# Top-k attention with a squared-ReLU feed-forward: the last batch by quarters, last rows two batches at a time, and attention ahead of older feed-forward work

## The chip, the cores and the metric

The kernel runs on one core of a Trainium2 chip. The metric is the time of one execution in device microseconds (us). A profile of one execution gives the span from the first to the last instruction, which is some microseconds shorter.

## The reference

There are 8 batches, 8 heads, 576 rows and a head width of 64. Each row of attention keeps its 32 largest scores; the result, with the heads side by side, goes through a feed-forward block of 512, 2048 and 512 columns.

```python
def _attn_ref(q, k, v):                       # (8, 8, 576, 64) each
    scores = np.matmul(q, k.transpose(0, 1, 3, 2)) / np.sqrt(64)
    kth = np.partition(scores, -32, axis=-1)[..., -32:-31]
    scores = np.where(scores >= kth, scores, -1000000000.0)
    attn = np.exp(scores - np.max(scores, axis=-1, keepdims=True))
    attn = attn / (np.sum(attn, axis=-1, keepdims=True) + 1e-09)
    return np.matmul(attn, v)

def reference(q, k, v, moe_w_in, moe_w_out):
    x = _attn_ref(q, k, v).transpose(0, 2, 1, 3).reshape(4608, 512)
    r = np.maximum(x @ moe_w_in, 0.0)         # w_in: 512 x 2048
    return (r * r) @ moe_w_out                # w_out: 2048 x 512
```

## The kernel before

**Groups.** Attention is done in 144 groups. A group is 128 query rows of two heads of one batch (a head pair, hp), or, for the rows 512 to 575 (called Z), 64 rows of four heads. A batch has 4 pairs with the row blocks 0 to 3, and two Z groups. For each group:

- TensorE makes the scores s in fp32 (two heads beside each other, 128 x 1152) and ScalarE copies them to SBUF (L541).
- VectorE and GpSimd find the 32nd largest score of each row. VectorE folds each row into the maximum of pairs, m (L597), and of fours, f (first quarter, L607); GpSimd makes the values that were left out by integer addition and subtraction of the bit patterns (L592): a small half of 144 columns (t2, then `mid`) and a large half of 288 columns (t1, then `low`). VectorE takes eight maxima and replaces them, three times over a growing part of f (L624, L628; the replacements need `mid`), and then eight of all of it (kth, L631, which needs `low`). kth is exact unless a check at the very end finds that a row did not fit; then everything is done again in a plainer way, which does not happen with these inputs.
- ScalarE makes a mask w from s and kth (L639), one instruction for each head. TensorE transposes s and adds the mask, scaled to a very large negative number, in PSUM; I call these 18 matmuls the flip. They are L433, tile `ident,s`, and L430, tile `steep_bf,w`. ScalarE takes the exponential (p, L673).
- `collect`, for one or two groups of a pair at once: TensorE multiplies p with v (av, with the sum of each row in a column of its own), ScalarE copies av (L700), VectorE takes the reciprocal of the sum (L702), GpSimd normalizes (x, L704), TensorE transposes x, and ScalarE copies it into its place in xt (L728).

**Chunks.** When all heads of a chunk of rows are in xt, `feed` does the feed-forward block for these rows: 64 first-layer matmuls (tile `xt,win` or `xz,win`), whose outputs fill PSUM banks of 512 columns each, Relu on ScalarE (g, L754), the square on GpSimd (L768) or ScalarE (L771), on VectorE for the last chunk (L765); then for each 128 rows 16 second-layer matmuls of 512 columns (tile `wo,g`), a copy (L788) and a store. Chunks are the rows 0 to 255 and 256 to 511 of a batch, and the last 64 rows of four batches together. The last batch begins with its Z groups, goes on with the row blocks 2 and 3 of all pairs as one chunk, and ends with block 0 and block 1 as chunks of 128 rows.

**The order of the work.** No engine's order is written out by hand. Each operation is handed to a planner with an assumed duration and a priority, a time at which it would be wanted (smaller is sooner). The planner plays the program through with these durations: on each engine, whenever it is free, it takes the ready operation with the smallest priority for which buffers are free. The order that results is fixed in the program; on the chip each engine goes through its own list, and waits on semaphores for what an instruction needs. Priorities are spaced by PER for each group (`tg = T0 + PER * n`). Scores are wanted LEAD before tg, the pair and four maxima ME and MQ before it, the small half MP before it, the flip and what follows at tt. Feed-forward work is wanted from the end of the chunk's attention plus NBO, spaced by STEP, and later by LAG (LAGL in the last batch).

Buffers that matter here: all short-lived PSUM tiles (av, transposes, both feed-forward layers) share two banks, named psum. Scores have three banks, the flip two and a part of a third, and that third bank is shared with a scratch tile of the maxima (sq). In SBUF there are 6 buffers of s, and 4 each of f, w and p.

The lines that set the row order, the chunks and the flip's priority:

```python
seq = [(0, Z), (2, Z)] + [(hp, g) for hp in range(NHP) for g in (2, 3)]   # last batch
return seq + [(hp, g) for g in (0, 1) for hp in range(NHP)], [[0], [1], [2, 3]]
...
if b % 4 == 3:
    CHUNKS.append([(b - 3 + i, 512, 64) for i in range(4)])
CHUNKS += [[(NB - 1, 256, 256)], [(NB - 1, 0, 128)], [(NB - 1, 128, 128)]]
...
tt = tg + PER + 2
```

Of the kernel before, what the change touches and what calls it, by code (L numbers as in the profile page):

```python
# [8 lines left out]
FP32 = mybir.dt.float32  # L9
BF16 = mybir.dt.bfloat16  # L10
I32 = mybir.dt.int32

P = 128
# [278 lines left out]
def bass_top_k_attn__then__act_relu_squared_kernel(  # L292
# [8 lines left out]
    NB, H, S, D = q.shape  # L301
# [4 lines left out]
    NHP = 4  # L306
    NPAIR = NB * NHP
    NBLK = 9
    DM = H * D
    DFF = moe_w_in.shape[1]  # L310
    NFB = DFF // P
    NCT = DM // P
    NALL = NPAIR * NBLK

    def sb(name, shape, dt=FP32, n=None):
# [1 line left out]
            return nc.alloc_sbuf_tensor(name, shape, dt)  # L317
        return [nc.alloc_sbuf_tensor(f"{name}{i}", shape, dt) for i in range(n)]

    PER = 5.52  # L320
    T0 = 12.0
    LEAD = 36.03
    ME = 17.74
    MQ = 18.56
    MP = 5.21
    MA = 21.03
    SQ = 4.72
    WD = 4
    WC = 0
    WA = 2.47  # L330
    WN = 6
    NBO = 8.74
    LAG = 12.01
    STEP = 2.91
    LATE = 1.54
    LAGL = 20

    ident32 = sb("ident32", [P, P])
    ident_bf = sb("ident_bf", [P, P], BF16)
# [3 lines left out]
    NGRP = NALL // 2  # L343
# [17 lines left out]
        "t2": ([P, 2, QUART], FP32, 2), "f": ([P, 2, S], FP32, 4), "a": ([P, 2, 8], FP32, 2),  # L361
        "sh": ([P, 2], FP32, 2), "w": ([P, 2, S], BF16, 4), "p": ([P, 9, 128], BF16, 4),
        "av": ([P, 4, D + 1], FP32, 3), "x": ([P, 4, D], BF16, 2), "xt": ([P, NCT, 256], BF16, 4),
        "xz": ([P, NCT, 256], BF16, 2), "o": ([P, DM], FP32, 2),
    }
    mem = {nm: sb(nm, *spec) for nm, spec in sizes.items()}
    pools = {nm: Pool(nm, spec[2]) for nm, spec in sizes.items()}
# [34 lines left out]

    Z = 4

    def batch_order(b):
        if b < NB - 1:
            seq = [(hp, g) for hp in range(NHP) for g in (0, 1)]
            for hp in range(NHP):
                seq += [(hp, 2), (hp, 3)] + ([(hp - 1, Z)] if hp % 2 else [])
            return seq, [[0, 1], [2, 3]]  # L410
        seq = [(0, Z), (2, Z)] + [(hp, g) for hp in range(NHP) for g in (2, 3)]
        return seq + [(hp, g) for g in (0, 1) for hp in range(NHP)], [[0], [1], [2, 3]]


    CHUNKS = []
    for b in range(NB):
        if b < NB - 1:
            CHUNKS += [[(b, 0, 256)], [(b, 256, 256)]]
        if b % 4 == 3:
            CHUNKS.append([(b - 3 + i, 512, 64) for i in range(4)])  # L420
    CHUNKS += [[(NB - 1, 256, 256)], [(NB - 1, 0, 128)], [(NB - 1, 128, 128)]]

    def two(ap, step, n_):

# [12 lines left out]
    def build(full, weights, pl):  # L437
        state = {"n": 0, "u": 0, "pairs": 0, "last": {}}
# [66 lines left out]
        def top_k(gi, qks, tg):  # L505

            n = state["n"]
# [54 lines left out]
            if full:  # L562
                a, sh = tile("a"), tile("sh")
                for rnd in range(4):
                    src = st if rnd == 0 else f
                    for i in range(2):
                        get = dict(r=[st]) if rnd == 0 else dict(hold=[f])
                        if rnd == 3:
# [4 lines left out]
                                       after=prev[i], take=[a] if rnd == 0 and i == 0 else [],  # L573
# [57 lines left out]
                    ks.append(chain(kth, i, prev[i] + [low], .665, lambda i=i: vec.max(  # L631
                        eighth(kth, i), at(f)[:, i, :]), hold=[f]))
            kths.extend(ks)
            tw = tg + PER
            wt = tile("w")
            if not full:

# [6 lines left out]
            for i in range(2):  # L644
                o = pl.op("gp", .75, tw + 1.3 * i, lambda i=i: gp.tensor_scalar(
                    at(f)[:, i, :], at(st)[:, i, :], kth[:, i, n:n + 1], STEEP, ALU.subtract, ALU.mult),
                    r=[st], hold=[f], after=[ks[i]])
# [86 lines left out]
        def feed(chunk, xt, tm, step):  # L734

            nt = sum(n_ for _, _, n_ in chunk)
            b = chunk[-1][0]
            last, end = b == NB - 1, chunk is CHUNKS[-1]
            kf = max(1, 512 // nt)
            lag = 0 if end else LAGL if last else LAG  # L740
            gs = [tile("g") for _ in range(NFB // kf)]
            for i, g in enumerate(gs):
                hh = Tile(psum)

                def fh(hh=hh, i=i):
                    for f in range(kf):
                        fb = kf * i + f
                        for ct in range(NCT):
                            ins = mm(bank(hh)[:, nt * f:nt * f + nt], win[:, ct, 128 * fb:128 * fb + 128],
                                     at(xt)[:, ct, 0:nt], ct == 0 and f == 0)  # L750
                    return ins

                def fr(hh=hh, g=g):
                    return act.activation(at(g)[:, 0:kf * nt], bank(hh)[:, 0:kf * nt], ACTF.Relu)  # L754

                tf = tm + step * i
                w_ = kf * nt
                ho = pl.op("pe", .03 + kf * 4 * (nt / 2340 + .002), tf + lag, fh, r=[xt], w=[hh], take=[hh, g],
                           after=weights if chunk is not CHUNKS[0] else weights and weights[NCT * (kf * i // 8):][:NCT],
                           nbf=tf if not last else 0)  # L760
                if chunk is CHUNKS[0] and weights:
                    first_h.append(ho)
                pl.op("act", .19 + w_ / 1200, tf + lag + .5, fr, r=[hh], w=[g])
                if end:
                    pl.op("dve", .1 + w_ / 1900, tf + lag + .8, lambda g=g: vec.tensor_tensor(  # L765
                        at(g)[:, 0:w_], at(g)[:, 0:w_], at(g)[:, 0:w_], ALU.mult), u=[g])
                elif last or i * SQ % 8 < SQ:
                    pl.op("gp", .15 + w_ / 480, tf + lag + 1, lambda g=g: gp.tensor_tensor(  # L768
                        at(g)[:, 0:w_], at(g)[:, 0:w_], at(g)[:, 0:w_], ALU.mult), u=[g])
                else:  # L770
                    pl.op("act", .19 + w_ / 1200, tf + lag + 1, lambda g=g: act.activation(  # L771
                        at(g)[:, 0:w_], at(g)[:, 0:w_], ACTF.Square), u=[g])
            for tb in range((nt + 127) // 128):
                n_ = min(128, nt - 128 * tb)
                op_, ob = Tile(psum), tile("o")
                to = tm + step * (len(gs) + 1 + 4 * tb)
                for sub in range(4):
                    def fo(sub=sub, op_=op_, tb=tb, n_=n_):
                        for fb in range(4 * sub, 4 * sub + 4):
                            c = nt * (fb % kf) + 128 * tb  # L780
                            ins = mm(bank(op_)[0:n_, :], at(gs[fb // kf])[:, c:c + n_], wo[:, fb, :], fb == 0)
                        return ins

                    pl.op("pe", .9, to + lag + step * sub, fo,
                          r=sorted({gs[fb // kf] for fb in range(4 * sub, 4 * sub + 4)}, key=lambda t: t.num),
                          w=[op_], take=[op_, ob] if sub == 0 else [], after=weights[8 + 2 * sub:10 + 2 * sub], order=[ho],
                          nbf=to + step * sub if not last else 0)
                pl.op("act", .6, to + lag + 4 * step, lambda op_=op_, ob=ob, n_=n_: act.copy(  # L788
                    at(ob)[0:n_, :], bank(op_)[0:n_, :]), r=[op_], w=[ob])
                rows, at_ = [], 0  # L790
                for b_, r0, m_ in chunk:
                    lo_, hi_ = max(at_, 128 * tb), min(at_ + m_, 128 * tb + n_)
                    if lo_ < hi_:
                        rows.append((lo_ - 128 * tb, hi_ - lo_, S * b_ + r0 + lo_ - at_))
                    at_ += m_
                pl.op("sp", 2.3, to + lag + 4 * step + 1, lambda ob=ob, rows=rows: [nc.sync.dma_start(
                    out[row:row + m_, :], at(ob)[p0:p0 + m_, :]) for p0, m_, row in rows],
                    r=[ob], ndma=len(rows), sem=lambda o: f"o{o.tiles[0].slot}")
# [13 lines left out]
        for b in range(NB):  # L812
            seq, stages = batch_order(b)
            pairs, held = {}, {}
            last = b == NB - 1
            for hp, gi in seq:
                tg = T0 + PER * state["n"]
                hps = (hp, hp if gi != Z else hp + 1)
                for x in hps:
                    if x not in pairs:  # L820
                        pairs[x] = load_pair(b, x, tg)
                st, wt = top_k(gi, [pairs[x][0] for x in hps], tg)
                tt = tg + PER + 2
                pt = attend(gi, st, wt, tt)
                js = [gi] if gi == Z else [g for g in stages if gi in g][0]
                held.setdefault((hp, js[0]), []).append((pt, [pairs[x][1] for x in hps]))
                if gi != js[-1]:
                    continue
                r0, n_ = 128 * js[0], 128 * len(js) if gi != Z else 64
                i, col = place(b, r0, n_)  # L830
                first = xts[i] is None
                if first:
                    xts[i] = tile("xz" if len(CHUNKS[i]) > 1 else "xt")
                collect(gi, held[hp, js[0]], (xts[i], col, first), hp, tt)
                left[i] -= n_ * (2 if gi == Z else 1)
                if left[i] == 0:
                    tm = T0 + PER * state["n"] + (NBO if not last else 8)
                    c = CHUNKS[i]
                    feed(c, xts[i], tm, (STEP if b < NB - 2 else 1.9) if not last else (1.5 if c is not CHUNKS[-1] else .5))
# [63 lines left out]
    early, pre, zeros, weights = setup(main)  # L903
# [3 lines left out]
    n = 0  # L907
# [79 lines left out]
```

## Time and profile before

| | before |
|---|---|
| time, median of 3 runs | 878.67 us (878.38 to 881.07) |
| span of the profile | 875.4 us |
| mean granted TensorE clock | 0.987 |
| busy: TensorE, VectorE, ScalarE, GpSimd | 809.3, 824.4, 765.1, 787.2 us |
| TensorE, second layer (`wo,g`, 128x512) | 379 ns mean of one |
| VectorE, kth (L631, 128x576) | 747 ns mean, 288 times |
| GpSimd, large half (L592, 128x576) | 1412 ns mean, 144 times |
| ScalarE, exponential (L673, 128x1152) | 1134 ns mean, 144 times |

In the profile PE is TensorE's matmuls and PEld its weight loads, DVE is VectorE, ACT is ScalarE, POOL is GpSimd, SPq is the queue that issues the transfers. The mean of one instruction is its whole duration: instructions overlap on their engine, so that a row of them takes less than their number times the mean. In a timeline a line holds several instructions of one kind that follow each other (x4); the number behind the start is the time from the start of the first to the end of the last. What stands in square brackets is idle time of the engine before the line, and what ended it. The change moves every line number after it by 14; the text names operations by their tiles.

### The profile page before, as it was taken

To read this page: it belongs to the slowest core of one execution; us is meant where nothing else is said; L and a number is where in the kernel's file an instruction comes from. 1 tells how busy PE (TensorE), PEld (TensorE's weight loads), DVE (VectorE), ACT (ScalarE), POOL (GpSimd) and SP (SyncE) were. 2 spreads that over 40 slices of the span, in tenths; PEclk is the share of its full clock that TensorE was granted. 3 is DMA by queue.
4 is the path that set the end of the run, shared out by engine and by line. 5 is a ranking of instruction groups with operands and counts; after the bars stand their busy time and mean duration, and the time that the engine had idled before them with its cause. 6 is when DMAs were issued, how large, how long until landed. Compare 5 with 4: busy or idle time off the path is not lost.

```text
span 875.4 us, 22041 instructions
## 1 busy us (share of the span) xinstructions
PE 809.3 (92%) x7726; PEld 608.3 (69%) x7778; DVE 824.4 (94%) x3409; ACT 765.1 (87%) x1254; POOL 787.2 (90%) x821
## 2 busy tenths in 40 slices
PE   4777999999999999998999999999999999999996
PEld 3556767667776777766677677776777676777674
DVE  2899999999999999999999999999999999999951
ACT  4798988899998998889989889898999899898873
POOL 6888999999999889998999969999999989999962
PEclk9699999999999999999999999999999999999999
DMA  8982112031210213011320032101321030000101
GB/s 182 214 217 76 42 28 55 16 86 35 70 42 13 68 34 90 16 52 28 70 68 2 13 90 65 48 16 40 81 57 42 13 82 15 26 2 25 26 13 41
DMA packets 126967, 48.18 MB, mean 55 GB/s; under 512 B 119168, under 2 KB 119168, under 8 KB 126848
## 3 DMA queue, kind: packets, MB, share of 16 engines
q1 hardware_dynamic: 125648, 46.39, 21.3%
q8 instruction: 63, 1.03, 0.5%
q14 instruction: 56, 0.46, 0.2%
q10 hardware_dynamic: 1200, 0.30, 0.2%
HBM read 37.22 MB, written 9.44 MB: 53 GB/s over the span
## 4 chain that ended last, share of the span: by engine, by line
DVE 59%; PE 23%; ACT 10%; issue 4%; POOL 2%; DMA 0%; SPq 0%; DVEq 0%
DVE f L628 19%; PE ps L430 16%; DVE c L624 14%; DVE kth L631 12%; PE ps L433 6%; DVE f L607 5%; DVE ps L597 4%; DVE m L597 4%; ACT p L673 3%; ACT s L541 3%; ACT w L639 2%; POOL f L592 1%; POOL t L592 1%; ACT g L754 1%; DMA rq<-in_q_dram 0%
## 5 line engine op out<-in xcount | busy, mean ns | idle before, releaser
L628 DVE MATCH_REPLACE8 f<-c,f 128x104 f32<-128x104 f32 (+2 forms) x864 | 267.0, 315 | 0.0
L624 DVE MAX8 c<-f 128x8 f32<-128x104 f32 (+2 forms) x864 | 244.9, 319 | 0.0
L433 PE MATMUL ps<-ident,s 128*128 128x128 f32 x1296 | 224.2, 282 | 20.5 <-ACT p L673 10.8
L639 ACT ACTIVATE w<-s,kth 128x576 bf16<-128x576 f32 x288 | 222.5, 783 | 15.7 <-DVE kth L631 14.5
L430 PE MATMUL ps<-qk 64*128 64x64 f32 (+3 forms) x1280 | 211.7, 450 | 16.8 <-DVE m L597 13.3
L592 POOL TENSOR_TENSOR t<-s 128x576 int32<-128x576 int32 x144 | 202.8, 1411 | 16.8 <-ACT s L541 16.6
L631 DVE MAX8 kth<-f 128x8 f32<-128x576 f32 x288 | 207.1, 747 | 1.3 <-POOL f L592 1.3
L592 POOL TENSOR_TENSOR f<-t,m 128x576 int32<-128x576 int32 x144 | 203.3, 1412 | 0.4
L430 PEld LDWEIGHTS ps<-qk 64*128 64x128 f32 (+1 forms) x1280 | 131.1, 179 | 93.5 <-issue 62.0
L541 ACT COPY s<-ps 128x1152 f32<-128x1152 f32 x144 | 161.6, 1122 | 27.2 <-PE ps L430 26.2
L673 ACT ACTIVATE p<-ps 128x1152 bf16<-128x1152 f32 x144 | 163.4, 1134 | 20.8 <-PE ps L430 19.3
L433 PEld LDWEIGHTS ps<-ident,s 128*128 128x128 f32 x1296 | 145.7, 142 | 49.1 <-ACT p L673 18.1
L430 PE MATMUL ps<-steep_bf,w 128*128 128x128 bf16 x1296 | 141.2, 221 | 0.0
L430 PE MATMUL ps<-wo,g 128*128 128x512 bf16 x524 | 129.3, 379 | 5.4 <-ACT g L754 1.7
L592 POOL TENSOR_TENSOR t<-m 128x288 int32<-128x288 int32 x144 | 114.9, 798 | 19.4 <-ACT m L605 13.8
L430 PE MATMUL ps<-xt,win 128*128 128x256 bf16 (+1 forms) x1088 | 126.5, 266 | 4.0 <-ACT g L754 1.7
L592 POOL TENSOR_TENSOR f<-t,f 128x288 int32<-128x288 int32 x144 | 114.8, 797 | 0.0
L768 POOL TENSOR_TENSOR g<-g 128x512 bf16<-128x512 bf16 x95 | 98.5, 1040 | 14.2 <-ACT g L754 12.5
L430 PEld LDWEIGHTS ps<-xt,win 128*128 128x128 bf16 x1088 | 96.6, 98 | 18.6 <-ACT g L754 3.3
L430 PEld LDWEIGHTS ps<-steep_bf,w 128*128 128x128 bf16 x1296 | 106.0, 100 | 4.8
L754 ACT ACTIVATE g<-ps 128x512 bf16<-128x512 f32 x144 | 84.7, 606 | 9.1 <-PE ps L430 8.2
L430 PEld LDWEIGHTS ps<-wo,g 128*128 128x128 bf16 x576 | 52.1, 98 | 49.5 <-ACT g L754 1.7
(60 smaller groups left out, 869.6 us busy)
## 6 DMA issues: line engine op xcount, KB each, us to landing
rq<-in_q_dram SPq DMA_DIRECT2D x64, 128.0 KB, 2.5
rv<-in_v_dram SPq DMA_DIRECT2D x64, 128.0 KB, 2.5
out_dram<-o SPq DMA_DIRECT2D x32, 256.0 KB, 2.1
rk<-in_k_dram SPq DMA_DIRECT2D x62, 128.0 KB, 2.6
g<-in_moe_w_in_dram SPq DMA_DIRECT2D x8, 512.0 KB, 4.8
g<-in_moe_w_out_dram SPq DMA_DIRECT2D x8, 512.0 KB, 4.2
rv<-in_v_dram SPq DMA_DIRECT2D x96, 16.0 KB, 2.3
rq<-in_q_dram SPq DMA_DIRECT2D x32, 32.0 KB, 2.7
```

The source lines that it names most:

```text
L430: return pe.matmul(o, l, r, start=start, stop=stop, skip_group_check=True)
L433: return pe.matmul(o, i, ident, is_transpose=True, skip_group_check=True, **kw)
L541: cp = [pl.op("act", 1.2, tg - LEAD + 1, lambda: act.copy(at(st)[:, :, :], two(banks(ss), SECOND, S)), r=[ss], w=[st])]
L592: return pl.op("gp", dur, prio, lambda: gp.tensor_tensor(o().bitcast(I32), x().bitcast(I32), y().bitcast(I32), op), **kw)
L597: return vec.tensor_tensor(o, two(banks(ss)[:, a:], SECOND + HALF, QUART), two(at(st)[:, 0, HALF + a:], HALF, QUART), ALU.max)
L624: lambda i=i, t=t, c0=c0, c1=c1: vec.max(eighth(t, i), at(f)[:, i, c0:c1]),
L628: lambda i=i, t=t, c0=c0, c1=c1: vec.match_replace(at(f)[:, i, c0:c1], eighth(t, i), at(f)[:, i, c0:c1], NEG), hold=[f])]
L631: ks.append(chain(kth, i, prev[i] + [low], .665, lambda i=i: vec.max(eighth(kth, i), at(f)[:, i, :]), hold=[f]))
L639: pl.op("act", .77, tw + .8 * i, lambda i=i: act.activation(at(wt)[:, i, :], at(st)[:, i, :], ACTF.Relu, bias=kth[:, i, n:n + 1], scale=-1.0),
L673: pl.op("act", 1.15, tt + 1, lambda: act.activation(at(pt)[:, :, :].rearrange("p k q -> p (k q)"), banks(e)[:, 0:2 * S], ACTF.Exp, scale=0 ...
L754: return act.activation(at(g)[:, 0:kf * nt], bank(hh)[:, 0:kf * nt], ACTF.Relu)
L768: pl.op("gp", .15 + w_ / 480, tf + lag + 1, lambda g=g: gp.tensor_tensor(at(g)[:, 0:w_], at(g)[:, 0:w_], at(g)[:, 0:w_], ALU.mult), u=[g])
```

## The change

The change cuts the feed-forward chunks smaller where they come due late, and sets new priorities. The last batch is handled by quarters: block 2, 3, 0 and 1 in turn over all pairs, each a chunk of 128 rows. The last 64 rows are gathered from two batches (128 rows) instead of four (256). The flip and what follows it get an earlier priority (TA), still earlier in the last NL groups (TL), so that attention goes ahead of feed-forward work of earlier rows. The other constants of the planner are set anew. A switch for quarters in the first batch (B0Q) is there but off. The durations that the planner assumes are left as they were.

```diff
-    PER = 5.52
+    PER = 5.55
-    LEAD = 36.03
-    ME = 17.74
-    MQ = 18.56
-    MP = 5.21
-    MA = 21.03
-    SQ = 4.72
-    WD = 4
-    WC = 0
-    WA = 2.47
+    LEAD = 40
+    ME = 16.41
+    MQ = 15.52
+    MP = 18.0
+    MA = 18.98
+    SQ = 5.15
+    TA = 7.2
+    TW = -0.14
+    TL = 8.0
+    NL = 28.07
+    WD = 3.33
+    WC = 1.75
+    WA = 1.13
-    NBO = 8.74
-    LAG = 12.01
-    STEP = 2.91
-    LATE = 1.54
-    LAGL = 20
+    NBO = 3.81
+    LAG = 11.28
+    STEP = 3.19
+    LATE = 2.38
+    LAGL = 11.07
...
-        "xz": ([P, NCT, 256], BF16, 2), "o": ([P, DM], FP32, 2),
+        "xz": ([P, NCT, 64 * 2], BF16, 2), "o": ([P, DM], FP32, 2),
...
+    B0Q, LQ, ZB = 0, 1, 2
...
-        seq = [(0, Z), (2, Z)] + [(hp, g) for hp in range(NHP) for g in (2, 3)]
+        seq = [(0, Z), (2, Z)]
+        if LQ:
+            return seq + [(hp, g) for g in (2, 3, 0, 1) for hp in range(NHP)], [[0], [1], [2], [3]]
+        seq += [(hp, g) for hp in range(NHP) for g in (2, 3)]
...
-        if b % 4 == 3:
-            CHUNKS.append([(b - 3 + i, 512, 64) for i in range(4)])
-    CHUNKS += [[(NB - 1, 256, 256)], [(NB - 1, 0, 128)], [(NB - 1, 128, 128)]]
+        if b % ZB == ZB - 1:
+            CHUNKS.append([(b - ZB + 1 + i, 512, 64) for i in range(ZB)])
+    CHUNKS += [[(NB - 1, 256, 128)], [(NB - 1, 384, 128)]] if LQ else [[(NB - 1, 256, 256)]]
+    CHUNKS += [[(NB - 1, 0, 128)], [(NB - 1, 128, 128)]]
...
-            tw = tg + PER
+            tw = tg + PER - TW
...
-                tt = tg + PER + 2
+                tt = tg + PER + 2 - TA - TL * max(0, 1 - (NGRP - state["n"]) / NL)
```

WA sets how many of the 16 weight casts go to ScalarE (12 before, 8 after), SQ how many of the squares go to GpSimd, WD and WC when weights are loaded and cast, MA when ScalarE copies a part of m, and LATE how long the planner holds back a reciprocal.

More of the change, by code (lines that the diff above doesn't have):

```diff
@@ L403, in bass_top_k_attn__then__act_relu_squared_kernel @@
     Z = 4
+    B0Q, LQ, ZB = 0, 1, 2
     def batch_order(b):
         if b < NB - 1:
-            seq = [(hp, g) for hp in range(NHP) for g in (0, 1)]
+            if b == 0 and B0Q:
+                seq = [(hp, g) for g in (0, 1) for hp in range(NHP)]
+            else:
+                seq = [(hp, g) for hp in range(NHP) for g in (0, 1)]
             for hp in range(NHP):
                 seq += [(hp, 2), (hp, 3)] + ([(hp - 1, Z)] if hp % 2 else [])
-            return seq, [[0, 1], [2, 3]]
-        seq = [(0, Z), (2, Z)] + [(hp, g) for hp in range(NHP) for g in (2, 3)]
+            return seq, [[0], [1], [2, 3]] if b == 0 and B0Q else [[0, 1], [2, 3]]
+        seq = [(0, Z), (2, Z)]
+        if LQ:
+            return seq + [(hp, g) for g in (2, 3, 0, 1) for hp in range(NHP)], [[0], [1], [2], [3]]
+        seq += [(hp, g) for hp in range(NHP) for g in (2, 3)]
         return seq + [(hp, g) for g in (0, 1) for hp in range(NHP)], [[0], [1], [2, 3]]
-    CHUNKS = []
-    for b in range(NB):
+    CHUNKS = [[(0, 0, 128)], [(0, 128, 128)], [(0, 256, 256)]] if B0Q else [[(0, 0, 256)], [(0, 256, 256)]]
+    for b in range(1, NB):
         if b < NB - 1:
             CHUNKS += [[(b, 0, 256)], [(b, 256, 256)]]
-        if b % 4 == 3:
-            CHUNKS.append([(b - 3 + i, 512, 64) for i in range(4)])
-    CHUNKS += [[(NB - 1, 256, 256)], [(NB - 1, 0, 128)], [(NB - 1, 128, 128)]]
+        if b % ZB == ZB - 1:
+            CHUNKS.append([(b - ZB + 1 + i, 512, 64) for i in range(ZB)])
+    CHUNKS += [[(NB - 1, 256, 128)], [(NB - 1, 384, 128)]] if LQ else [[(NB - 1, 256, 256)]]
+    CHUNKS += [[(NB - 1, 0, 128)], [(NB - 1, 128, 128)]]
+    FIRST = CHUNKS[:2 if B0Q else 1]
     def two(ap, step, n_):
@@ L758, in feed @@
                 ho = pl.op("pe", .03 + kf * 4 * (nt / 2340 + .002), tf + lag, fh, r=[xt], w=[hh], take=[hh, g],
-                           after=weights if chunk is not CHUNKS[0] else weights and weights[NCT * (kf * i // 8):][:NCT],
+                           after=weights if chunk not in FIRST else weights and weights[NCT * (kf * i // 8):][:NCT],
                            nbf=tf if not last else 0)
-                if chunk is CHUNKS[0] and weights:
+                if chunk in FIRST and weights:
                     first_h.append(ho)
```

## The prediction

> **What bounds the kernel now.** I read the page first (busy shares and slices), then the windows by stage, and last the timeline of the last 40 us.
>
> ```profile
> PE 809.3 (92%) x7726; PEld 608.3 (69%) x7778; DVE 824.4 (94%) x3409; ACT 765.1 (87%) x1254; POOL 787.2 (90%) x821
> PE   4777999999999999998999999999999999999996
> DVE  2899999999999999999999999999999999999951
> ```
>
> ```profile
> core 0: us, PE busy (x) PEld busy (x) DVE busy (x) ACT busy (x) POOL busy (x), PEclk, DMA share, GB/s
> 100.00:500.00 400.00, 375.50 (x3652) 282.57 (x3674) 398.32 (x1646) 362.12 (x591) 375.68 (x380) 1.00 0.17 43
> 500.00:700.00 200.00, 197.23 (x1897) 148.41 (x1910) 199.94 (x836) 184.28 (x305) 186.88 (x188) 1.00 0.20 49
> 775.00:840.00 65.00, 63.79 (x598) 47.59 (x601) 65.00 (x276) 55.94 (x92) 61.04 (x63) 1.00 0.07 18
> 850.00:860.00 10.00, 9.53 (x123) 7.30 (x122) 1.33 (x6) 5.23 (x11) 4.25 (x6) 1.00 0.08 28
> ```
>
> VectorE is full from 100 to 840 us: 398.32 of 400 us, then 65.00 of 65. So the middle runs at VectorE's pace, about 5.7 us for each of 144 groups. Its missing 51 us (875.4 - 824.4) lie at the two ends: some 21 us before 100 us, 2 us in the middle, and some 28 us after 840 us. The end is the place to look.
>
> ```profile
> 836.11 1.42 DVE L631 MAX8 kth<-f 128x8 f32<-128x576 f32 x2
> 839.43 1.04 POOL L768 TENSOR_TENSOR g<-g 128x512 bf16<-128x512 bf16 x1 [1.18 <-ACT g L754]
> 839.71 0.79 ACT L639 ACTIVATE w<-s,kth 128x576 bf16<-128x576 f32 x1
> 840.36 0.44 DVE L628 MATCH_REPLACE8 f<-c,f 128x272 f32<-128x272 f32 x1
> 840.78 1.40 POOL L592 TENSOR_TENSOR t<-s 128x576 int32<-128x576 int32 x1
> 842.14 1.04 POOL L768 TENSOR_TENSOR g<-g 128x512 bf16<-128x512 bf16 x1
> 843.49 1.40 POOL L592 TENSOR_TENSOR f<-t,m 128x576 int32<-128x576 int32 x1
> 844.92 1.42 DVE L631 MAX8 kth<-f 128x8 f32<-128x576 f32 x2 [1.34 <-POOL f L592]
> 846.29 0.61 PE L433 MATMUL ps<-ident,s 128*128 128x128 f32 x4
> 846.65 0.78 ACT L639 ACTIVATE w<-s,kth 128x576 bf16<-128x576 f32 x1
> 850.18 0.63 PE L433 MATMUL ps<-ident,s 128*128 128x128 f32 x4
> 865.40 3.40 PE L430 MATMUL ps<-wo,g 128*128 128x512 bf16 x15
> 868.84 0.58 ACT L788 COPY o<-ps 128x512 f32<-128x512 f32 x1 [2.86 <-PE ps L430]
> ```
>
> Two things happen here. First, VectorE has finished the last group's replacements at 840.8 but starts its final maximum at 844.92: GpSimd made the missing half (843.49) only after squares of feed-forward work (L768) queued ahead of it. One reciprocal of 0.17 us lies between, so 3.9 us are lost. Second, the flip of group 142 (the transposes of s) has its mask w at 840.50, and starts at 846.29; that of group 143 has w at 847.43 and starts at 850.18. TensorE is full, and other work is in front. Followed back through the timeline, flips start 3 to 5 us after their kth up to 480 us, but 13 us after it around 810 to 835 us. So the end is TensorE's: from the last flip at 850.18 to 868.8 it has 18.6 us of nearly unbroken work.
>
> **What the skill says.** "Perfetto Trace Analysis", Identifying the Most-Contended Engine: occupancy is a fair measure for Vector, and a poor one for Tensor. The trace agrees: PE shows 94% before 500 us and 98% from 500 to 700, and around 705 us flips keep up (4 us) all the same. "TensorE: Matmul & The Clock Gate", Back-to-back issue gap, gives N/2.4 + 2.5 ns when warm: 56, 109 and 216 ns for 128, 256 and 512 columns. The starts in this trace are 56, 109 and 216 ns apart; the same section's 81 ns (128) for streams with weight loads is not seen here: 48 such loads took 2.68 us. So splitting a 256-column matmul into two costs 2 x 56 - 109 = 3 ns. "GPSIMD Engine Reference", Elementwise — side-by-side cycle accounting, has GpSimd about twice as slow as VectorE on tensor_tensor; here the square takes 1040 ns on GpSimd and 426 ns on VectorE, so squares weigh on the queue that the last group needs.
>
> **The change part by part.** The programs of both kernels fix the order on every engine; I compare these orders and price them with the trace: a transpose of s 0.110 us, a matmul of 128, 256 or 512 columns 0.056, 0.109 or 0.216 us, a group of four score matmuls 1.28 us.
>
> 1. *Smaller chunks (ZB, LQ).* Three 256-row chunks' worth of first-layer matmuls are cut in two: 192 more matmuls, 192 x 3 ns = 0.6 us of TensorE. The 16 second-layer matmuls per 128 rows stay. The last batch is gathered by quarters: four more reciprocals (some 0.1 us each, 0.4 us on VectorE, which is on the path), and 8 small instead of 4 large av, x and xt operations: 0.7 us more on GpSimd (8 x 0.397 - 4 x 0.614), 1.3 us on ScalarE, beside other work.
> 2. *What they move.* 128 rows cost TensorE 64 x 0.056 + 16 x 0.216 = 7.0 us. With chunks of two batches, one such portion falls due at batch 1 instead of 3 and another at batch 5 instead of 7, so one less waits for the last batch. Summing the two orders up to each flip, the changed kernel has done 8 us more feed-forward work at flip 78, the same at 84 to 110, 4 us more at 114, 12 us at 131, and 3.6 us more at flip 143. There is room for it: around 480 us flips lag only 5 us, and the pile-up of 15 us that follows (four batches of last rows at once) goes.
> 3. *Attention earlier (TA, TL, NL).* tt falls by 7.2, and by up to 8 more in the last 28 groups, so flips pass older feed-forward work, while NBO, LAG and LAGL let that work start earlier. This adds no operation. The 13 us lag before the end should fall to 2 to 4 us.
> 4. *The other constants.* They move weight casts (ScalarE 12 to 8, GpSimd 4 to 8 at 1.04 us) and squares (GpSimd 95 to 92, ScalarE 45 to 48), and the halves from GpSimd earlier (MP). GpSimd gains 4.2 - 3.1 + 0.7 = 1.8 us in all, hidden: it is at 90%. The first 20 instructions on VectorE keep their order, and the transfers wait for the same casts to within 1 us, so I put the start at nothing, plus or minus 1.5 us.
> 5. *The last group.* In the new GpSimd order the last large half stands before the squares, so the 3.9 us wait goes. Instead the small half (f<-t,f) of group 143 stands behind a normalization and a square. VectorE has 3.5 us of work between what that half needs and its use. GpSimd can start the normalization 1.9 us into it, and needs 0.4 + 1.0 + 0.8 us and three handovers of some 0.1: 4.3 us, so 0.8 us of waiting. Queued behind that wait on VectorE is the whole last selection, and flip 143 waits for it. Its bounds are 0 (the square is done earlier) and 2 us (another square ahead); I take 0.8.
>
> Now the end. Last kth before: 846.3. Minus 3.9, plus 0.4, plus 0.8: 843.6. The two masks follow with an exp (1.13 us) and small copies between them: flip 143 at about 845.8. TensorE must have got through 743.1 us of priced work by then. From flip 126 (658.8 us; kth at 747.4, so about 750.5), at the ratio of time to price that before shows from flip 120 to 143 (130.9 us for 122.4, or 1.07), it arrives at 840.7; from flip 120 it arrives at 846. So TensorE is just in time. After flip 143 the old order holds 17.9 us of priced work (the trace: 18.6), the new one 15.5: 8 second-layer and 16 first-layer matmuls fewer, one av more. With the same 0.7 us of gaps, 845.8 + 16.2 = 862.0 against 868.8. That is 6.8 us less; I take 6.5, as TensorE is only just in time. 878.67 - 6.5 = 872.2 us.
>
> **The rivals.**
> - *A wait takes the place of the one removed.* GpSimd's small half, or ScalarE with exp before mask, holds VectorE in several of the last groups (the work that hides the small half is 3.5 to 7 us there, 5.6 to 12.7 before). For it: GpSimd is at 61.04 of 65 us there. Against: the half itself goes first in most groups. 2 us in the selection and 2 us in the masks leave the 2.4 us of TensorE: 876.2 us.
> - *VectorE loses its pace in the middle: slower.* Flips first may delay scores, or squares the halves. A loss of 0.07 us a group over 144 groups is 10 us; less 6.5, 882 us. Against it: the scores stand as many groups ahead of each flip in both orders (to within one), and VectorE lost only 2 us in 740.
> - *The start improves too.* The 21 us before 100 us hold waits of some 5 us between groups, for the bank shared by sq and e9. Earlier flips may halve it (2.7 us) and the last group's 0.8 and some of the gaps may go (2 us): 867.5 us.
> - *TensorE is full from 480 us to the end in both.* Then moving work buys nothing and the time is the same, 879 us. Against it: lag fell from 15 to 4 us between 510 and 705 us, so there was slack to fill. I count it with the first.
>
> **How the numbers follow.** Forecast 0.64; wait in place 0.17 (about half of it within 0.3%, over 876.0); slower 0.09; start too 0.10. Faster: 0.64 + 0.10 + 0.08 = 0.82; same 0.09; slower 0.09. The range takes the better start and the wait in its place, 867.5 to 877.0, and leaves the slower case out.
>
> **What would show it.** Right: no wait of over 1 us of the last kth for GpSimd; flips within some 4 us of their kth after 780 us; some 16 us from the last flip to TensorE's end; VectorE still full from 100 to 840. Wrong: VectorE idle of over 4 us in the middle, flips that still lag by 10 us, or a last flip later than 848.

## The result and the profile after

The changed kernel takes 871.02 us (median of 4 runs, 870.55 to 872.77), beside 878.52 us for the kernel before in the same set (877.55 to 881.07): a ratio of 0.9914, with a 95% interval of 0.9889 to 0.9939. Measured once more beside the last experiments it gave 0.9926 (0.9899 to 0.9953). The span of the profile falls from 875.4 to 869.0 us.

From the page, the busy times and the slices of TensorE and VectorE:

```profile
PE 809.9 (93%) x7911; PEld 612.7 (71%) x7970; DVE 822.5 (95%) x3413; ACT 760.3 (87%) x1261; POOL 788.2 (91%) x826
PE   5777999989999999998999999999999999999996
DVE  2989999999999999999999999999999999999971
```

The same stages in the windows:

```profile
core 0: us, PE busy (x) PEld busy (x) DVE busy (x) ACT busy (x) POOL busy (x), PEclk, DMA share, GB/s
100.00:500.00 400.00, 384.62 (x3783) 290.91 (x3809) 399.99 (x1669) 364.70 (x598) 380.23 (x384) 1.00 0.18 45
500.00:700.00 200.00, 194.15 (x1912) 146.84 (x1927) 199.91 (x831) 185.10 (x308) 190.13 (x193) 1.00 0.19 47
775.00:840.00 65.00, 63.50 (x704) 49.13 (x710) 64.01 (x270) 56.54 (x100) 62.54 (x67) 1.00 0.06 18
850.00:860.00 10.00, 9.62 (x110) 6.81 (x109) 2.87 (x9) 4.65 (x10) 3.48 (x5) 1.00 0.08 28
```

Hardly any sum of work has changed: TensorE +0.6 us, VectorE -1.9, GpSimd +1.0. What changed is when it is done. TensorE is busy 9 us more from 100 to 500 us, and VectorE is now full there (399.99 of 400 us). The end, from the timeline:

```profile
835.39 0.80 POOL L606 TENSOR_TENSOR f<-t,f 128x288 int32<-128x288 int32 x1
836.23 0.09 DVE L642 MATCH_VALUE_LOAD f<-c,f 128x8 f32 x1 [0.83 <-POOL f L606]
838.82 0.43 DVE L642 MATCH_REPLACE8 f<-c,f 128x272 f32<-128x272 f32 x1
839.17 1.41 DVE L645 MAX8 kth<-f 128x8 f32<-128x576 f32 x2
841.79 0.78 ACT L653 ACTIVATE w<-s,kth 128x576 bf16<-128x576 f32 x1
845.96 0.60 PE L447 MATMUL ps<-ident,s 128*128 128x128 f32 x4
854.91 3.74 PE L444 MATMUL ps<-xt,win 128*128 128x128 bf16 x64
858.70 3.40 PE L444 MATMUL ps<-wo,g 128*128 128x512 bf16 x15
862.13 0.59 ACT L802 COPY o<-ps 128x512 f32<-128x512 f32 x1 [2.86 <-PE ps L444]
```

The last kth follows its replacements without a wait (839.17). In the place of the old wait stands one of 0.83 us for the small half. The last kth is done at 840.6 us (846.3 before), the flip of group 143 starts at 845.96 (850.18), the second layer ends at 862.1 (868.8).

I read all runs below by a table of three stretches: from kth of group 42 to kth of 137 (the middle), from there to kth of 143 (the last six groups), and from there to the end of the span (the tail), all in us and from one trace of each kernel. All that differs in the start, before about 270 us, drops out of it. Where kth of 137 stands in VectorE's order differs between kernels (in e1 it comes late), so that some us can move between the middle and the last six; their sum does not depend on it. "Ratio" is that of the times to the kernel before, the start included.

| kernel | ratio | kth 42 at | middle | last six | tail |
|---|---|---|---|---|---|
| before | 1 | 270.5 | 539.8 | 36.0 | 29.1 |
| after | 0.9914 | 270.3 | 537.1 | 33.1 | 28.5 |
| after, again (e11) | 0.9926 | 274.3 | 537.1 | 33.1 | 28.0 |
| e8 chunks alone | 1.0008 | 270.6 | 542.1 | 34.1 | 29.2 |
| e4 chunks, TA, TL, old constants | 0.9970 | 271.3 | 539.1 | 31.8 | 32.7 |
| e3 chunks, new constants, no TA, TL | 0.9987 | 272.4 | 538.4 | 36.6 | 29.5 |
| e12 after without TL | 0.9946 | 272.5 | 536.8 | 34.9 | 29.9 |
| e2 after, block 2 and 3 as one chunk | 0.9926 | 272.1 | 537.1 | 33.7 | 29.1 |
| e1 after, last rows of four batches | 1.0101 | 270.3 | 547.4 | 29.2 | 36.0 |
| e5 before, large half first | 1.0005 | 268.6 | 539.8 | 33.1 | 32.6 |
| e6 after, 5.3 us less TensorE at 780 | 0.9940 | 272.1 | 537.1 | 33.1 | 28.6 |
| e7 the same at 650 | 0.9948 | 273.2 | 537.5 | 33.1 | 28.3 |
| e9 the same after 840 | 0.9926 | 268.5 | 537.0 | 33.1 | 30.7 |
| e10 after, 6 us less VectorE | 0.9886 | 270.2 | 533.7 | 33.1 | 28.8 |

So the change gained 2.7 us in the middle, 2.9 in the last six groups and 0.6 in the tail: 6.2 of 604.9 us. The trace of after, taken again, repeats each stretch to within 0.5 us, although its span is 3.5 us longer: the difference lies before kth 42.

The windows from kth 42 to kth 143, before and then after, show what was gained ahead of the tail:

```profile
270.60:846.30 575.70, 554.51 (x5359) 416.30 (x5395) 570.04 (x2371) 520.01 (x857) 535.87 (x542) 1.00 0.17 41
270.40:840.60 570.20, 552.85 (x5489) 416.76 (x5534) 569.10 (x2376) 518.12 (x864) 534.82 (x543) 1.00 0.17 43
```

VectorE's busy time hardly differs (570.04 and 569.10 us), but its idle time falls from 5.7 to 1.1 us. Of the 5.7 us before, 3.9 stand in front of the last kth; of the 1.1 us after, 0.83.

### The profile page after: what moved, and what is told of

The parts are those of the page before. It is cut to its first block, busy times and chain, and to the rows that moved or that the text cites. A ratio compares the mean times of both kernels' runs of the same rounds, so it can differ in the third digit from the quotient of the medians.

```text
span 869.0 us, 22447 instructions
## 1 busy us (share of the span) xinstructions
PE 809.9 (93%) x7911; PEld 612.7 (71%) x7970; DVE 822.5 (95%) x3413; ACT 760.3 (87%) x1261; POOL 788.2 (91%) x826
## 4 chain that ended last, share of the span: by engine, by line
DVE 64%; PE 17%; ACT 11%; issue 4%; POOL 1%; DMA 1%; SPq 0%; DVEq 0%
DVE f L642 21%; DVE c L638 16%; PE ps L444 13%; DVE kth L645 13%; DVE f L621 5%; PE ps L447 5%; DVE ps L611 5%; DVE m L611 4%; ACT s L555 3%; ACT p L687 3%; ACT w L653 1%; ACT g L768 1%; POOL f L606 1%; POOL t L606 1%; DVE rzall L716 1%
## 5 line engine op out<-in xcount | busy, mean ns | idle before, releaser
L642 DVE MATCH_REPLACE8 f<-c,f 128x104 f32<-128x104 f32 (+2 forms) x864 | 272.2, 325 | 0.0
L638 DVE MAX8 c<-f 128x8 f32<-128x104 f32 (+2 forms) x864 | 248.8, 329 | 0.0
L447 PE MATMUL ps<-ident,s 128*128 128x128 f32 x1296 | 223.1, 281 | 21.5 <-ACT p L687 14.7
L444 PE MATMUL ps<-qk 64*128 64x64 f32 (+3 forms) x1280 | 214.2, 454 | 10.2 <-DVE m L611 8.8
L606 POOL TENSOR_TENSOR t<-s 128x576 int32<-128x576 int32 x144 | 202.5, 1411 | 13.2 <-ACT s L555 13.1
L645 DVE MAX8 kth<-f 128x8 f32<-128x576 f32 x288 | 209.5, 757 | 0.0
L555 ACT COPY s<-ps 128x1152 f32<-128x1152 f32 x144 | 161.5, 1121 | 34.7 <-PE ps L444 33.7
L606 POOL TENSOR_TENSOR t<-m 128x288 int32<-128x288 int32 x144 | 115.0, 799 | 19.3 <-ACT m L619 14.7
L782 POOL TENSOR_TENSOR g<-g 128x512 bf16<-128x512 bf16 x92 | 95.7, 1042 | 12.9 <-ACT g L768 11.7
L611 DVE TENSOR_TENSOR ps<-ps,s 128x288 f32<-128x288 f32 x144 | 66.6, 462 | 22.1 <-ACT s L555 17.1
```

Of the source, the lines that this page charges most:

```text
L444: return pe.matmul(o, l, r, start=start, stop=stop, skip_group_check=True)
L447: return pe.matmul(o, i, ident, is_transpose=True, skip_group_check=True, **kw)
L555: cp = [pl.op("act", 1.2, tg - LEAD + 1, lambda: act.copy(at(st)[:, :, :], two(banks(ss), SECOND, S)), r=[ss], w=[st])]
L606: return pl.op("gp", dur, prio, lambda: gp.tensor_tensor(o().bitcast(I32), x().bitcast(I32), y().bitcast(I32), op), **kw)
L611: return vec.tensor_tensor(o, two(banks(ss)[:, a:], SECOND + HALF, QUART), two(at(st)[:, 0, HALF + a:], HALF, QUART), ALU.max)
L638: lambda i=i, t=t, c0=c0, c1=c1: vec.max(eighth(t, i), at(f)[:, i, c0:c1]),
```

## The experiments

Each expectation is quoted as it was written before the run. Theory A is the one I held at the time, and it changes with what the runs showed.

**Undoing one part of the change.**

```diff
# e1
-    B0Q, LQ, ZB = 0, 1, 2
+    B0Q, LQ, ZB = 0, 1, 4
-        "xz": ([P, NCT, 64 * 2], BF16, 2), ...
+        "xz": ([P, NCT, 256], BF16, 2), ...
# e2
-    B0Q, LQ, ZB = 0, 1, 2
+    B0Q, LQ, ZB = 0, 0, 2
# e3
-    TA = 7.2
-    TL = 8.0
+    TA = 0
+    TL = 0
# e4: every other constant as before (PER 5.52, LEAD 36.03, ... LAGL 20, TW 0)
```

> The changed kernel with the last 64 rows gathered from four batches again (ZB 4, xz of 256 columns), all else as changed. Theory A (TensorE sets the end, and feed-forward work that falls due sooner fills its slack before 500 us): one portion of 128 rows, 7.0 us of TensorE, comes back into the last batch, and the pile-up near 510 us too: 4 to 7 us slower than the changed kernel, 875 to 878 us. Theory B (flips ahead of older feed-forward work are the gain): the flips keep their priority, within 1.5 us of the changed kernel, 870 to 872.5 us.

e1: 888.53 us, ratio 1.0101 (1.008 to 1.0121), much slower than the 875 to 878 us of theory A. A likely cause is that with the new lags feed-forward work starts sooner, and that TensorE runs out of it where a chunk falls due only once in four batches. From the windows of e1:

```profile
280.00:285.00 5.00, 3.96 (x44) 3.31 (x42) 5.00 (x21) 4.74 (x8) 3.21 (x5) 1.00 0.37 105
285.00:290.00 5.00, 3.67 (x44) 2.81 (x44) 5.00 (x21) 4.00 (x7) 4.14 (x4) 1.00 0.38 85
```

TensorE is busy for 7.63 of 10 us here (9.63 in after). VectorE is full, so nothing is lost yet. At kth 143 e1 is 6.4 us behind after, with a wait of 2.87 us of VectorE for GpSimd's small half at 841.3 us, and its tail is 7.5 us longer. So the small chunk is needed by the new constants; that the idle TensorE of these windows is the reason was not tested by itself.

> The changed kernel with the last batch's rows 256 to 511 as one chunk again (LQ 0). Theory A: TensorE has 18.0 us of priced work after the last flip instead of 15.6, and the first quarter's feed-forward work falls due four groups later: 1 to 3 us slower than the changed kernel, 872 to 874 us. Theory B: the flips come as before, within 1 us, 870 to 872 us.

e2: 873.70 us, ratio 0.9926 (0.991 to 0.9943). The time is within theory A's range, but the ratio is that of after itself in e11, so the whole time does not tell e2 from after. The stretches lean to theory A: the last six groups and the tail are 1.2 us longer together, 18.0 us of priced TensorE work stand behind the last flip instead of 15.6, and the last kth has a wait of 1.67 us for GpSimd again.

> The changed kernel with TA and TL at 0: the flip and what follows it wanted at the old time, so that they stand behind older feed-forward work. Theory A: the same work in another order, and even less of it after the last flip (12.6 us of priced work instead of 15.6): within 1.5 us of the changed kernel, 870 to 872.5 us. Theory B: most of the gain is lost, 4 us or more slower, 875 us or more.

e3: 878.22 us, ratio 0.9987 (0.9974 to 1.0). Theory A is wrong here: without TA and TL nearly all of the gain is lost. The timeline of VectorE in e3 shows how:

```profile
759.92 0.09 DVE L642 MATCH_VALUE_LOAD f<-c,f 128x8 f32 x1 [1.98 <-POOL f L606]
813.64 0.09 DVE L642 MATCH_VALUE_LOAD f<-c,f 128x8 f32 x1 [1.86 <-POOL f L606]
```

Twice VectorE stands for 2 us before its first replacements, for the small half from GpSimd. Neither wait is in after. But neither is in the kernel before, which has no wait for a small half of over 0.15 us from 100 us on: these waits come with the new constants, and TA and TL keep them away. They are not what the change gained over the kernel before.

> The changed kernel with every constant that the old one has at its old value (PER, LEAD, ME, MQ, MP, MA, SQ, WD, WC, WA, NBO, LAG, STEP, LATE, LAGL; TW 0), and the chunks, TA, TL and NL as changed. Theory A: chunks carry most, the constants the small waits of VectorE in the middle (2.9 us) and the order of the end (19.7 us of priced work after the last flip): 2 to 4 us slower than the changed kernel, 873 to 875 us. A third theory, that the constants carry most: 876 us or more.

e4: 877.02 us, ratio 0.997 (0.9952 to 0.9989). By the number this is the third theory, that the constants carry most; but e3 has the constants, and keeps still less of the gain. The stretches tell the parts apart. Up to the last kth e4 is nearly as fast as after (570.9 us, 570.2 in after, 575.0 in e3): this is the part of TA and TL. But 19.7 us of priced TensorE work stand behind the last flip, and the tail is 3.6 us longer than before and 4.2 longer than after: this is the part of the constants.

> The changed kernel with TL = 0: no extra advance of attention in the last 28 groups, TA stays. Theory A: what was lost without TA and TL (the time from kth 42 to kth 143 was 575.0 instead of 570.2 us, with two waits of 2 us for GpSimd's small half at 758 and 812 us) was lost by the last groups' order; then TL = 0 brings most of it back, 874 to 877 us. Theory B: TA's 7.2 us do it for all groups and TL adds little: within 1 us of the changed kernel.

e12: 875.45 us, ratio 0.9946 (0.9931 to 0.9962). The time is in theory A's range, yet only 1.4 us over the 874.09 us of after in the same set (e11), with intervals that overlap. The stretches decide for theory A: TL is worth 2.9 us by them, 1.8 of them in the last six groups.

**The parts alone.**

```diff
# e8: the new chunks in the kernel before: constants as before, TA = TL = TW = 0
# e5: the kernel before, with t1 and low of the last group wanted 30 us sooner
-                whole(1.38, tg, ALU.add, lambda: at(t1)[:, :, :], ...
-                low = whole(1.38, tg + 2, ALU.subtract, ...
+                whole(1.38, tg - (30 if n == NGRP - 1 else 0), ALU.add, ...
+                low = whole(1.38, tg + 2 - (30 if n == NGRP - 1 else 0), ...
```

> The changed kernel with old constants and TA and TL at 0, so that only the chunks are changed. If the parts add up (without early attention 7.9 us and with old constants 5.9 us more span than the changed kernel): a span of 880 to 884 us, slower than before (875.4). If the chunks carry the gain alone: a span of 870 to 873 us. If early attention and constants only repair the same thing: 876 to 878 us.

e8: 878.95 us, ratio 1.0008 (0.9991 to 1.0025): no difference. The span of 876.0 us is the third number of the expectation, but its reading, that early attention and constants repair the same thing, does not fit: undoing either loses nearly as much as undoing both, so each needs the other. The chunks do take the last group's wait of 3.9 us away, to waits of 1.0 us, and the last six groups gain 1.9 us; but the middle is 2.3 us longer, with waits of VectorE for the copy of the scores (1.64 us at 745.9 us and 1.00 at 764.0).

> The kernel before, with the two GpSimd operations of the last group's large half (t1 and low) wanted 30 us sooner, ahead of the squares. The prediction's step (the 3.9 us wait of VectorE is on the path): the last kth and the end come 3 to 4 us sooner, 874.5 to 875.5 us where before has 878.5. Theory A (TensorE's queue sets the end): the last kth comes some 3 us sooner, but the last flip keeps its place behind other work, and the time falls by 1 us at most.

e5: 878.17 us, ratio 1.0005 (0.9984 to 1.0025): no difference either, and this is the run that tests the largest single step of the prediction. From the timeline of e5, the large half comes early:

```profile
837.12 1.42 POOL L592 TENSOR_TENSOR f<-t,m 128x576 int32<-128x576 int32 x1
```

The last six groups take 2.9 us less, as hoped, and the tail 3.5 us more: flip 143 starts at 848.1 instead of 850.2, 6.5 us after its kth instead of 3.9. TensorE came 0.3 us sooner to it, counted from kth 42: from 837 to 848 us its instructions follow each other without a wait of over 0.1 us. Its priced work behind the flip was 18.3 us, 18.0 before. Once the wait of 3.9 us was taken away, TensorE's queue took its place.

**Less work on one engine.** e6, e7 and e9 leave out three first-layer matmuls of four and three second-layer matmuls of four in one chunk each, e10 the large half in the last maximum of ten groups.

```diff
# e6, e7, e9: cond = last rows of batches 6 and 7; of 4 and 5; block 0 of batch 7
-                        for ct in range(NCT):
+                        for ct in range(1 if cond else NCT):
-                        for fb in range(4 * sub, 4 * sub + 4):
+                        for fb in range(4 * sub, 4 * sub + (1 if cond else 4)):
# e10
-                        eighth(kth, i), at(f)[:, i, :]), hold=[f]))
+                        eighth(kth, i), at(f)[:, i, 0:HALF] if n in range(45, 136, 10) else at(f)[:, i, :]), hold=[f]))
```

> The changed kernel with most feed-forward work of the last chunk of last rows (batches 6 and 7) left out: only one of four parts of each sum is made, in both layers, so these 128 rows are wrong. 48 + 12 matmuls, 5.3 us of TensorE, go from the stretch near 780 to 805 us; the planned order stays as it is. Theory A: the flips after it come some 5 us sooner, until VectorE holds them; the last flip can't start before its mask (842.6 in the changed kernel, the flip 846.0): 2.5 to 4 us faster than the changed kernel, a span of 865 to 866.5 us. A rival (VectorE and GpSimd set the end): within 1 us of the changed kernel, a span of 868 to 870 us.

> The same for the chunk of last rows of batches 4 and 5, whose feed-forward work lies near 650 to 700 us. Theory A: there TensorE has slack before the pile-up that begins at about 725 us, and the 5.3 us are gone by then: within 1 us of the changed kernel, a span of 868 to 869.5 us. If TensorE were full from 500 us to the end: as much as with the late chunk, 3 us or more faster.

e6: 874.34 us, ratio 0.994 (0.9923 to 0.9957); e7: 874.11 us, 0.9948 (0.9931 to 0.9965). Neither is faster than after, and the stretches equal its own to within 0.4 us. In e6 the flip of group 134 starts 13.4 us after its kth (14.7 in after), that of group 136 13.1 us in both: the gain is gone two groups later. The timeline of TensorE in e6 shows into what:

```profile
798.12 0.33 PE L447 MATMUL ps<-ident,s 128*128 128x128 f32 x1 [0.55 <-DVE f L621]
808.20 0.23 PE L447 MATMUL ps<-ident_bf,x 128*128 128x128 bf16 x1 [1.16 <-ACT o L802]
808.65 0.33 PE L447 MATMUL ps<-ident,s 128*128 128x128 f32 x1 [0.23 <-DVE f L621]
```

TensorE waits 3.7 us from 775 to 815 us, where after waits 0.5; half of it is with the ninth transpose of a flip. That one goes to the bank shared with the maxima's scratch tile, and VectorE frees it with a later group's maxima of fours (L621). So the flips are tied to VectorE's pace. Theory A of these runs, that TensorE's amount of work counts, is wrong up to about 805 us.

> The changed kernel, with the last maxima (kth) of every tenth group from group 45 to 135 taken over the first 288 columns only instead of 576, so that in ten groups the threshold is not searched in the large half. That takes 10 x 2 x 0.3 = 6.0 us off VectorE, spread thinly, and nothing off any other engine. Theory A: from 270 us to the last kth VectorE's own work sets the pace, as two kernels with 5.3 us less TensorE work in that stretch, and no gain between 270 us and the end, suggest; then it is 4 to 6 us faster than the changed kernel (ratio to before about 0.986), and the time between the kth of groups 42 and 143 falls from 570.2 to about 565 us. Theory B: TensorE or GpSimd is the bound there as well, at 97% and 95% busy; then less than 2 us come of it, and VectorE shows idle time in its place.

e10: 869.98 us, ratio 0.9886 (0.9862 to 0.991), beside 0.9926 (0.9899 to 0.9953) for after on the same chip; the intervals overlap. The middle is 3.4 us shorter, which lies between the two theories. From the groups by line and shape of e10, 270 to 830 us, with the waits behind the last bar:

```profile
L611 DVE TENSOR_TENSOR ps<-ps,s 128x288 f32<-128x288 f32 x98 | 45.3, 463 | 1.5 <-ACT s L555 0.7
L645 DVE MAX8 kth<-f 128x8 f32<-128x288 f32 x20 | 8.7, 463 | 0.0
```

VectorE's own work sets the pace, but not by much: the shorter maxima take 6.0 us off it (20 starts 0.3 us closer), and part comes back as waits in front of the pair maxima, 1.5 us in all instead of 0.2.

> The changed kernel, with one first-layer matmul of four and one second-layer matmul of four left out in the chunk of the last batch's block 0 (the chunk before the last; those rows come out incomplete). That takes 48 x 0.056 + 12 x 0.216 = 5.3 us of TensorE's work out of the stretch from about 840 to 855 us, and moves nothing else. Theory A: from about 820 us to the end TensorE's amount of work sets the time; then it is 4 to 5 us faster than the changed kernel (ratio to before about 0.986), and most of it shows in the time from the last flip to the end. Theory B: after the last flip the chain through exponential, av, copies, normalization and transpose to the last chunk's first layer (8.95 us from flip 143 to that layer in the changed kernel) sets the time, and the other feed-forward work only fills its gaps; then only the 1.7 us of it that stands between the last mask and the last flip counts, and it is 1 to 2 us faster (ratio about 0.990).

> The changed kernel itself, beside its variants on one chip. 0.9914 of before was measured first; all readings of the others are against this one. If the time before 270 us is what differs from run to run, the span less the time of kth 42 is 598.7 us again, to within 0.3 us, whatever the span is.

e9: 873.15 us, ratio 0.9926 (0.9901 to 0.995), and e11, after itself: 874.09 us, also 0.9926. To take 5.3 us off TensorE's last 25 us gains nothing. The windows of e9 show that something else happened:

```profile
846.00:850.00 4.00, 1.87 (x26) 1.17 (x24) 1.17 (x5) 3.24 (x6) 2.18 (x3) 0.97 0.00 0
850.00:856.00 6.00, 4.99 (x39) 3.98 (x40) 0.42 (x1) 1.55 (x4) 1.56 (x3) 0.50 0.13 46
856.00:858.00 2.00, 2.00 (x31) 2.00 (x31) 0.58 (x2) 1.09 (x2) 0.00 (x0) 0.85 0.00 0
```

and its timeline:

```profile
851.62 0.29 PE L447 MATMUL ps<-ident_bf,x 128*128 128x128 bf16 x1 [0.74 <-POOL x L718]
852.26 5.80 PE L444 MATMUL ps<-xt,win 128*128 128x128 bf16 x64
858.12 3.40 PE L444 MATMUL ps<-wo,g 128*128 128x512 bf16 x15
```

TensorE was busy for 1.87 of 4 us, then the granted clock (third number from the end) fell to 0.50, and the last first layer took 5.80 us instead of 3.74. Without these 2.06 us e9's tail would be 28.6 us, as in after. From flip 143 to that first layer it is 8.18 us in e9 and 8.95 in after: exponential, av, two copies, normalization and transpose, with the squares that GpSimd does between them in both kernels, set that time (theory B). The feed-forward matmuls that e9 leaves out cost under 1 us there; with them the granted clock stayed at 1.00 from 850 to 860 us.

## Why the prediction was right, point by point

The forecast was 872.2 us (867.5 to 877.0) against 871.02, but two of its steps were off, in opposite directions, and in part the number is right by luck.

1. *Smaller chunks, 0.6 us of TensorE and 0.4 us of VectorE.* Consistent, no more: the chunks alone change the time by +0.08%, too little to resolve such sums.
2. *What they move.* Right as to what happens: at group 84 the flip starts 4.5 us after its kth, not 14.8, so the pile-up is gone. The prediction gave these steps no worth of their own; the runs put it at nothing alone (e8) and at 14 us with the new constants (e1: 612.6 us in the three stretches against 598.7).
3. *Attention earlier: flip lag from 13 to 2 to 4 us.* Wrong as to how. In after the lag is still 13 to 15 us from group 123 to 137, and 5.4 us at 143; flips that still lag by 10 us were a sign of being wrong that the prediction named. I took the lag for a queue on TensorE at 98% busy; e6 and e7 show that less work on TensorE does not shorten it for more than a few groups. What TA and TL did instead is keep VectorE from waiting: with the new chunks they shorten the time from kth 42 to the last kth by 5.3 us under the old constants (576.2 to 570.9, e8 and e4) and by 4.8 under the new ones (575.0 to 570.2, e3 and after, where 4.3 us were waits for small halves). Through which buffers earlier flips do this was not shown.
4. *The start within 1.5 us.* Not contradicted: kth 42 comes at 270.5 us before and at 270.3 and 274.3 us in the two traces of after, which differ among themselves by more than that.
5. *The last group.* The wait of 0.8 us for the small half is there, with 0.83 us, and the step itself was right: kth 142 is done 2.5 us sooner than before, kth 143 5.8 us sooner, 3.3 us for the last group. The last kth was put at 843.6 and came at 840.6. The term mis-sized is what is not the last group: I had carried the middle over unchanged, plus 0.4 us, and it came 2.5 us shorter. Of this 1.4 us are starts of VectorE that came later than usual after the one before (2.3 us before, 0.9 after, summed from 270 to 830 us; the largest part is maxima of fours, which need ScalarE's copy of a part of m); the rest is not accounted for. TA and TL, which the prediction had costed by the flips' lag alone, shorten this time as point 3 says; the other constants shorten it by 1.2 us without them (e8 to e3) and by 0.7 with them (e4 to after). Which of the constants does that was not tried.
6. *The end: flip 143 at 845.8, 16.2 us behind it.* Measured: 845.96 and 16.2. The flip was on time only because the error of point 5 (3 us sooner) and that of point 3 (a lag of 5.4 us, not 2.2) cancel. That is the luck in the number. And e5 shows that the step "minus 3.9" is worth nothing where 18 us stay behind the last flip. A shorter selection and less work behind the flip pay together: from e8, TA and TL alone bring 1.8 us of the stretches (e4: 5.3 us up to the last kth, less 3.5 in the tail), the constants alone 0.9 (e3), both 6.7.

The rival "TensorE is full from 480 us to the end" falls with e6 and e7, up to some 805 us. "A wait takes the place of the one removed" is what e5 shows in the kernel before. "VectorE loses its pace in the middle" did not come: the middle is 2.7 us shorter.

The Trainium skill's page "Perfetto Trace Analysis", Identifying the Most-Contended Engine, which the prediction cited, held better than the prediction's own use of it: VectorE's 95% was the bound (e10), TensorE's 97 to 98% was not (e6, e7). I quoted it for the middle, and still read the end as TensorE's from 98% busy.

What stays open: in the tail of after, GpSimd does two squares (851.04, 2.21 us) before the normalization of the last group (853.22), whose reciprocal was there at 850.75. VectorE, with 2.87 of 10 us busy there, could do squares at 0.42 us each. This was not tried. The last flip of after also still stands in TensorE's queue: its mask is done at 842.57 us and it starts at 845.96. e9 takes 0.7 us of matmuls out of that queue and the flip comes no sooner after its kth, as TensorE then waits 0.70 us for the copy of an output; no run took out more there. No version tried that does all the work beats after.

## What to carry to other kernels

When two engines are both nearly full, take some microseconds of work off each in turn, in a stretch of its own: here the one that binds paid 3.4 of 6.0 us, the other nothing of 5.3. A wait at the end is worth what remains once the next queue is counted, so follow the last item to the end of the kernel with the wait gone before costing it. Two sets of priorities were worth 1.8 and 0.9 us each by itself here and 6.7 us together; test them in pairs before dropping one.

## What the runs showed of the hardware

- TensorE's clock fell to half in the tail of e9 after 4 us at 47% busy, in which no wait was longer than 1.3 us, and came back 4.4 us after steady work began: matmuls of 128 columns started 107 ns apart from 852.3 to 856.7 us, then 56 ns. The Trainium skill, "TensorE: Matmul & The Clock Gate", Part 1: The HAM clock gate, tells of half rate after an idle window of about 3.4 us and of full rate after about as long a busy one. The ratio and the order of the times agree; in this one trace the window needed not be idle, only half so.
- The two traces of after differ before 270 us, not later. The windows of after, and of after again:

```profile
34.00:44.00 10.00, 8.59 (x44) 6.22 (x44) 9.68 (x36) 8.36 (x15) 8.97 (x10) 0.66 0.72 187
190.00:200.00 10.00, 8.02 (x89) 6.58 (x87) 10.00 (x44) 8.80 (x19) 9.57 (x9) 1.00 0.47 106
```

```profile
34.00:44.00 10.00, 7.71 (x28) 5.19 (x29) 8.30 (x32) 7.47 (x14) 7.84 (x9) 0.58 0.66 167
190.00:200.00 10.00, 8.37 (x68) 6.55 (x69) 10.00 (x44) 7.10 (x15) 9.49 (x10) 0.83 0.52 118
```

The granted clock is lower in both windows of the second (0.58 and 0.83), and its kth 42 comes 4.0 us later; whether the clock is the cause was not tested. All later stretches agree to 0.5 us, so a stretch-by-stretch reading can tell differences of 1 us apart where the whole time, with 5.5 us between the runs of e11, does not.
